# Range checks moved from the recurrence into the second MoE, on a second load

## The chip, the cores and the metric

One core of a Trainium2 chip. The time of a run is the device time of that core in microseconds (us). The engines are TensorE (PE in the profile; PEld are its weight loads), VectorE (DVE), ScalarE (ACT), GpSimd (POOL) and SyncE (SP), which here issues every DMA. All work in float32; matrix products of the two MoEs split each operand into a rounded part and a remainder, so that one product becomes several passes of TensorE.

## The reference, cut to what matters

Three stages follow one another. The first is a recurrence over 768 time steps for 4 x 8 heads with a state of 40 x 40. Then come an MLP with an ELU (here called the first MoE; its weights arrive as 64-bit floats) and a soft mixture of 8 experts.

```python
for t in range(S):                       # recurrence, S = 768
    y[t] = einsum('bhd,bhde->bhe', r[t], state)
    Sa = einsum('bhde,bhe->bhd', state, a[t])
    state = state * w[t] - outer(Sa, b[t]) + outer(v[t], k[t])
h = x @ w_in                             # first MoE: 3072 tokens, 320 -> 2048 -> 320
x = where(h > 0, h, exp(min(h, 0)) - 1) @ w_out
P = sinkhorn(exp(x @ w_gate), 8 rounds)  # second MoE: 8 experts, 320 -> 1024 -> 320
out = sum_e P[:, e] * (relu(x @ w1[e]) @ w2[e])
```

## The kernel before, in words

**The recurrence** works in 24 chunks of 32 time steps. Chunk c loads w and a together as `WA` (`loadw`, line 290), k and b as `KE` (`loadk`), v as `VU` (`loadv`) and r as `rB` and `rO` (`loads2`). `prep` makes the decays of the chunk from w: two clamped copies (lines 315 and 316), two scans on VectorE (319, 325), and on GpSimd the product `aE` of a with them (327). Its last step is a range check of w on ScalarE: `Abs` with a bias and `Relu` with an accumulated sum, in place in the w half of `WA` (338, 339), summed into `wmm`. `WA` has one buffer (chunk 1 has one of its own), so the next load of w waits for the last reader. `E1` to `E4`, `H1` to `H4` and `O1` to `O3b` are matrix products and transposes of a chunk with the copies behind them. `E3` writes a 32 x 32 matrix for each head to memory (`Ad`, four stores, line 384), `LT` loads it back spread over the partitions (392).

**The triangular solve** (`tsolve`, lines 417 and 424) handles two chunks at a time with 62 short VectorE operations (`Tt`, `Wk`). It needs `LT` of both chunks; its result goes through memory again (`Td`, line 430, and `TT`, 434).

**The first MoE** runs unit by unit between the steps of the recurrence: `m1_mm1` (588), an ELU on ScalarE, VectorE and GpSimd, `m1_mm2` (615 to 619). Its weights are converted early on: 16 + 16 tiles, loaded as 64-bit words into two `raw` buffers (211, 221). `to_f32` turns the two 32-bit halves of a float64 into a float32: `Abs` on ScalarE (197), a clamp on VectorE that keeps the exponent in range (198), a shift (199) and two merges with words of the raw tile (200, 201).

**The second MoE** (`phase_b`) is 8 experts x 6 blocks x 8 slices = 384 units: `mm1` (773), `hh` on ScalarE (776), `hl` on VectorE (777), and two units later `mm2` (814 to 816). Weights come through a ring of 11 tiles (`wload`, 732 to 742), three units ahead of their use at a change of expert; one block of x at a time through `xload`. `gates` and `check_w`, which turns `wmm` into the flag, are spread over the first expert's units. At the end the flag selects a general version of the whole computation, which does not run with these inputs.

**What sets the order.** The tile framework orders the instructions of each engine by priority. For the loop over chunks the string `order` in `PLAN` gives the sequence of steps (`prep+4` is the next step of `prep` for chunk c + 4, `m` a unit of the first MoE, `p` three steps of the solve); from c = 4 on each engine follows it exactly. `start` gives the steps ahead of the loop. SyncE issues DMAs in order, so one that waits for a free buffer holds those behind it.

Of the kernel before, what the change touches and what calls it, by code (L numbers as in the profile page):

```python
# [22 lines left out]
PLAN = {  # L23
# [76 lines left out]
def build(ctx, tc, r, k, v, w, a, b, w_in, w_out, wg, w1, w2, wa_d, kb_d, re_d, ro_d, vt_d, wp_d, consts, out, C, off):  # L100
    nc = tc.nc
    B, H, S, D = r.shape
    DM = H * D
    NT = B * S
    NCH = S // C
    NG = H // 2
# [44 lines left out]
    flag = per.tile([1, 1], I32, name="flag")  # L151
    main = ExitStack()
    moe = ExitStack()
    rec = ExitStack()
# [37 lines left out]

    dve = {}

    def to_f32(raw, tmp):
        lo, hi, m = raw[:, :, 0], raw[:, :, 1], tmp.bitcast(I32)
        A.activation(out=tmp, in_=hi.bitcast(F32), func=AF.Abs)
        V.tensor_scalar(out=tmp, in0=tmp, scalar1=XLO, scalar2=XHI, op0=ALU.max, op1=ALU.min)
        V.tensor_scalar(out=m, in0=m, scalar1=3, scalar2=0x3FFFFFF8, op0=ALU.logical_shift_left, op1=ALU.bitwise_and)
# [52 lines left out]
    wmm = per.tile([128, NCH + 2], F32, name="wmm")  # L252
    wmid, whalf = wmm[:, NCH:NCH + 1], wmm[:, NCH + 1:NCH + 2]
    CI = C // 4

    work = {None: (wr, wq, dq, aB)}
# [1 line left out]
    def rec_init():  # L258
        for t in (wr, wq, dr, dq):
            V.memset(t, 0.0)  # L260
        work[1] = (early(1, "wr", [4 * NG, C + 1]), early(1, "wq", [4 * NG, C]), early(1, "dq", [4 * NG, C]), early(1, "aB", [NG * 2 * 2, 64]).rearrange("p (g u j) t -> p g u j t", u=2, j=2))
        for t in work[1]:
            G.memset(t, 0.0)
        V.memset(dr[:, :, 0], 1.0)
        for i in (3, 2):
            V.memset(bank[i], 0.0)
        for t in (aB, wmm, rB, *TTs, Yw):
            G.memset(t, 0.0)
        G.memset(wmid, -(WLO + WHI) / 2)
        G.memset(whalf, 1e-5 - (WHI - WLO) / 2)  # L270
        for i in (0, 1):
            V.memset(bank[i], 0.0)

# [35 lines left out]
    def prep(c):  # L309
        z = st[c]  # L310
        NX = 4 * NG
        wr, wq, dq, z.aB = work.get(c, work[None])
        wf = z.WA[0:HR, 0].rearrange("p g t -> p (g t)")
        wv = wf.rearrange("p (x t) -> p x t", x=NX)
        V.tensor_scalar(out=wr[0:HR, :, 1:C + 1], in0=wv[:, :, ::-1], scalar1=WLO, scalar2=WHI, op0=ALU.max, op1=ALU.min)
        V.tensor_scalar(out=wq[0:HR, :, 1:C], in0=wv[:, :, 0:C - 1], scalar1=WLO, scalar2=WHI, op0=ALU.max, op1=ALU.min)
        yield
        F = early(c, "F", [NX, C + 1])
        V.tensor_tensor_scan(out=flat(F)[0:HR], data0=flat(wr)[0:HR], data1=flat(dr)[0:HR], initial=0.0, op0=ALU.mult, op1=ALU.add)
        z.Wf = r2.tile([128, NX], F32, tag="Wf", name="Wf", bufs=4)  # L320
# [12 lines left out]
        kv = z.KE[0:HR].rearrange("p g u (b k t) -> p (g u b) k t", b=2, k=2)  # L333
        fr = F[0:HR, :, 0:C][:, :, ::-1]
        for kb in range(2):
            G.tensor_tensor(out=kv[:, :, kb, :], in0=kv[:, :, kb, :], in1=fr, op=ALU.mult)
        yield
        A.activation(out=wf, in_=wf, func=AF.Abs, bias=wmid[0:HR])
        A.activation(out=wf, in_=wf, func=AF.Relu, bias=whalf[0:HR], accum_out=wmm[0:HR, c:c + 1])

    def unpad(dst, ps):
        return dst.rearrange("p (j g e) -> p j g e", j=2, g=NG), ps.rearrange("p (g x) -> p g x", g=NG)[:, :, 0:128].rearrange("p g (j x) -> p j g x", j=2)[:, :, :, 0:D]
# [360 lines left out]
    def check_w(c1, px_tile):  # L703
        mm = c1.tile([128, 1], F32, name="mmw")
        V.tensor_reduce(out=mm, in_=wmm[:, 0:NCH], axis=AX.X, op=ALU.add)
        V.tensor_scalar(out=mm, in0=mm, scalar1=0.0, scalar2=None, op0=ALU.is_le)
        yield
        ps = px_tile()
        T.transpose(ps[0:1, 0:128], mm, ident)
        mn = c1.tile([1, 1], F32, name="mnw")  # L710
        V.tensor_reduce(out=mn, in_=ps[0:1, 0:128], axis=AX.X, op=ALU.min)
        V.tensor_scalar(out=mn, in0=mn, scalar1=-1.0, scalar2=1.0, op0=ALU.mult, op1=ALU.add)
        V.tensor_copy(out=flag, in_=mn)
        yield


# [4 lines left out]
    def phase_b(mg):  # L721
# [110 lines left out]
        for i in range(len(units) + LAG):  # L832
            if i < len(units):
                e, bk, f = units[i]
                if e == 0 and f == 2 and bk + 1 < NBLK:
                    xload(bk + 1)
                if i >= 2:
                    mm1(e, bk, f)
            if i >= LAG:
                e, bk, f = units[i - LAG]  # L840
                if gg is not None and e == 1:
                    run_all(gg)
                    gg = None
                mm2(e, bk, f)
                if bk == NBLK - 1:
                    del ring[(e, f)]
                    wnext()
            if gg is not None:
                if next(gg, 1) == 1:
                    gg = None  # L850


    def general():
        with ExitStack() as fx:
# [52 lines left out]
            for i in range(NF1):  # L907
                fs = slice(128 * i, 128 * i + 128)
                es = slice(128 * i * e32, (128 * i + 128) * e32)
                raw = f2.tile([128, 3, 128, e32], I32 if wide else F32, tag="fraw", name="fraw")  # L910
                SY.dma_start(out=raw[:, 0:2].rearrange("p k f e -> p k (f e)"), in_=wi_d[0:256, es].rearrange("(k p) f -> p k f", p=128))
                SY.dma_start(out=raw[0:64, 2].rearrange("p f e -> p (f e)"), in_=wi_d[256:320, es])
                SY.dma_start(out=raw[64:128, 2].rearrange("p f e -> p (f e)"), in_=wi_d[256:320, es])
                rv = raw.rearrange("p k f e -> p (k f) e")
                x = to_f32(rv, f2.tile([128, 384], F32, tag="cv", name="cv")) if wide else rv[:, :, 0]
# [278 lines left out]
```

## Time and profile before

| | us |
|---|---|
| median of 3 runs (lowest, highest) | 2324.01 (2320.37, 2327.19) |
| the profiled execution's own time | 2325.87 |
| its span, first to last instruction | 2323.8 |
| busy: PE, PEld, DVE, ACT, POOL | 2149.5, 1960.3, 989.1, 752.8, 469.2 |
| mean granted TensorE clock | 0.978 |

The span is what the views of the profile cover; the execution's own time is 2 us longer. A row of the timeline gives start, duration, engine, line, operation, the tiles out<-in, and in brackets the idle time ahead of it and what ended that.

### The profile page before, as it was taken

What the parts mean: (1) busy time and instruction counts of PE and PEld (TensorE: products, weight loads), DVE (VectorE), ACT (ScalarE), POOL (GpSimd) and SP (SyncE); (2) the same over time, 40 slices, a digit from 0 to 9 for tenths busy, and PEclk for the clock granted to TensorE, in tenths of its full rate; (3) what the DMA queues carried; (4) which work ended last, traced back from release to release, by engine and by line L of the source; (5) the groups of instructions that cost most, each with busy time, mean ns of one, the idle gap of its engine ahead of it and who ended that gap; (6) DMA issues with size and microseconds to landing.
All of it is one profiled execution on the core that took longest, in us unless ns stands there. A gap on an engine that the chain in (4) does not pass through costs nothing.

```text
span 2323.8 us, 47093 instructions
## 1 busy us (share of the span) xinstructions
PE 2149.5 (93%) x19908; PEld 1960.3 (84%) x19908; DVE 989.1 (43%) x2112; ACT 752.8 (32%) x1663; POOL 469.2 (20%) x556
## 2 busy tenths in 40 slices
PE   2377799999999999999999999999999999999998
PEld 2266788888888998899999999999999999999997
DVE  6788666676777622542222222222222222222222
ACT  3243345555555556323212112112112112112111
POOL 5244133433443326001002002002002002001000
PEclk9987799999999999999999999999999999999999
DMA  6344334433344223101001001001001001000000
GB/s 161 97 134 121 82 95 102 107 100 84 102 107 108 65 53 111 61 1 34 17 1 39 12 1 40 11 1 45 7 1 45 6 1 48 4 1 20 23 24 25
DMA packets 171588, 121.62 MB, mean 52 GB/s; under 512 B 102824, under 2 KB 151336, under 8 KB 171368
## 3 DMA queue, kind: packets, MB, share of 16 engines
q1 hardware_dynamic: 171368, 118.52, 19.0%
q8 instruction: 158, 2.59, 0.5%
q14 instruction: 62, 0.51, 0.1%
HBM read 99.99 MB, written 18.48 MB: 51 GB/s over the span
## 4 chain that ended last, share of the span: by engine, by line
PE 74%; DVE 11%; DMA 8%; SPq 2%; ACT 2%; issue 2%; POOL 1%; DVEq 0%; ACTq 0%; POOLq 0%
PE h L773 30%; PE pa L816 9%; PE pa L815 9%; PE pa L814 9%; PE ph L588 5%; DVE Wk L424 3%; DVE Tt L417 2%; DMA LT<-Ad 2%; PE a L615 2%; DMA Ad<-Am 2%; DMA WA<-in_wa 1%; PE a L616 1%; PE a L617 1%; DMA raw<-in_wp 1%; PE P L545 1%
## 5 line engine op out<-in xcount | busy, mean ns | idle before, releaser
L773 PE MATMUL h<-xs,a 128*128 128x512 f32 x2560 | 640.9, 392 | 0.0
L777 DVE SCALAR_TENSOR_TENSOR hl<-h,hh 128x512 fp32r<-128x512 f32 x384 | 264.8, 690 | 870.2 <-ACT hh L776 869.7
L776 ACT ACTIVATE hh<-h 128x512 fp32r<-128x512 f32 x384 | 229.4, 598 | 1015.3 <-PE h L773 1011.7
L773 PEld LDWEIGHTS h<-xs,a 128*128 128x128 f32 x2560 | 469.1, 188 | 82.7
L815 PE MATMUL pa<-a,hl 128*128 128x320 f32 x1536 | 474.4, 309 | 0.0
L814 PE MATMUL pa<-a,hh 128*128 128x320 f32 x1536 | 472.6, 309 | 0.6 <-ACT logits L643 0.3
L816 PE MATMUL pa<-a,hh 128*128 128x320 f32 x1536 | 468.6, 309 | 0.0
L815 PEld LDWEIGHTS pa<-a,hl 128*128 128x128 f32 x1536 | 289.0, 188 | 15.0
L814 PEld LDWEIGHTS pa<-a,hh 128*128 128x128 f32 x1536 | 289.0, 188 | 14.2 <-ACT acc L821 0.7
L816 PEld LDWEIGHTS pa<-a,hh 128*128 128x128 f32 x1536 | 287.3, 188 | 0.0
L741 POOL TENSOR_TENSOR a<-rw,a 128x384 fp32r<-128x384 f32 x64 | 65.2, 1019 | 1050.7 <-ACT a L739 1037.2
L588 PE MATMUL ph<-X,Wt 128*128 128x256 f32 x1536 | 236.1, 298 | 5.8 <-DVE g L597 5.7
L601 POOL TENSOR_TENSOR gl<-g,gh 128x256 fp32r<-128x256 f32 x192 | 161.8, 843 | 392.8 <-ACT gh L599 302.0
L588 PEld LDWEIGHTS ph<-X,Wt 128*128 128x128 f32 x1536 | 205.3, 198 | 10.9 <-DVE g L597 7.0
L424 DVE TENSOR_TENSOR Wk<-Wk,Tt 128x120 f32<-128x120 f32 (+30 forms) x403 | 160.0, 397 | 9.4 <-DVE Tt L417 0.2
L597 DVE SCALAR_TENSOR_TENSOR g<-m,ph 128x256 f32<-128x256 f32 x192 | 80.0, 416 | 163.0 <-ACT m L591 144.1
L417 DVE TENSOR_TENSOR Tt<-Wk,LT 128x120 f32<-128x120 f32 (+30 forms) x403 | 130.6, 324 | 37.8 <-DMA LT<-Ad 14.2
L825 DVE SCALAR_TENSOR_TENSOR acc<-pa,Pg,acc 128x320 f32<-128x320 f32 x168 | 84.3, 544 | 114.3 <-PE pa L816 114.3
L773 PE MATMUL h<-X,a 128*128 128x512 f32 x512 | 127.8, 392 | 0.0
L599 ACT ACTIVATE gh<-g 128x256 fp32r<-128x256 f32 x192 | 80.0, 417 | 143.9 <-DVE g L597 142.7
L590 ACT ACTIVATE m<-ph 128x256 f32<-128x256 f32 x192 | 73.0, 380 | 140.2 <-PE ph L588 132.8
L773 PEld LDWEIGHTS h<-X,a 128*128 128x128 f32 x512 | 93.7, 188 | 16.7
(173 smaller groups left out, 2437.2 us busy)
## 6 DMA issues: line engine op xcount, KB each, us to landing
LT<-Ad SPq DMA_DIRECT2D x24, 512.0 KB
rw<-in_moe_w SPq DMA_DIRECT2D x64, 160.0 KB
WA<-in_wa SPq DMA_DIRECT2D x24, 416.0 KB
KE<-in_kb SPq DMA_DIRECT2D x24, 416.0 KB
rw<-in_moe_w SPq DMA_DIRECT2D x64, 128.0 KB
VU<-in_vt SPq DMA_DIRECT2D x24, 320.0 KB
raw<-in_wp SPq DMA_DIRECT2D x16, 384.0 KB
raw<-in_moe_w_out SPq DMA_DIRECT2D x16, 320.0 KB
```

What stands on the lines that cost most here:

```text
L417: V.tensor_tensor(out=tv, in0=Wk[:, :, 0:ni, j:j + 1].to_broadcast(sh), in1=LT2[:, :, j, j + 1:C].unsqueeze(2).to_broadcast(sh), op=ALU.mult,)
L424: dve["T"] = V.tensor_tensor(out=Wk[:, :, 0:ni, j + 1:C], in0=Wk[:, :, 0:ni, j + 1:C], in1=tv, op=ALU.subtract)
L588: T.matmul(ph, lhsT=Wt[0:kp, wi, 128 * f:128 * f + 128], rhs=X[0:kp, xi, :], start=(i == 0), stop=(i == 7))
L597: V.scalar_tensor_tensor(out=g, in0=m, scalar=-1.0, in1=ph, op0=ALU.add, op1=ALU.max)
L601: G.tensor_tensor(out=gl, in0=g, in1=gh.bitcast(F32), op=ALU.subtract)
L773: T.matmul(h, lhsT=a1[:, wi, :], rhs=X[bk][:, xi, :], start=(i == 0), stop=(i == 7))
L776: A.activation(out=hh, in_=h, func=AF.Relu)
L777: V.scalar_tensor_tensor(out=hl, in0=h, scalar=0.0, in1=hh.bitcast(F32), op0=ALU.max, op1=ALU.subtract)
L814: T.matmul(o, lhsT=hh[:, ts_], rhs=a2[:, 0, :], start=(f == 0), stop=False)
L815: T.matmul(o, lhsT=hl[:, ts_], rhs=a2[:, 0, :], start=False, stop=False)
L816: T.matmul(o, lhsT=hh[:, ts_], rhs=a2[:, 1, :], start=False, stop=(f == NF2 - 1))
L825: V.scalar_tensor_tensor(out=at, in0=o, scalar=Pg[:, tt, e:e + 1], in1=at, op0=ALU.mult, op1=ALU.add)
```

## The change

The check of w leaves `prep`, and with it `wmm`. The conversion of the weights in the fast path no longer takes the absolute value and no longer clamps; its shift reads the raw word directly (the general version keeps both, as `guard`). A new generator, `check_ranges`, loads w (24 tiles) and the first MoE's weights (32 tiles) a second time during the second MoE and checks them on ScalarE, one step a unit from the second expert on; its result is put on one partition by two small DMAs in place of a transpose on TensorE. In `order` the step `ldw+4` behind `prep+3` becomes `ldw+5` behind O2, and `ldw_6` is added to `start`.

```diff
-"order": "T lv E4 m prep+3 ldw+4 p E3+3 xl m ... YW+1 prep+4 p O2 x m O2 p ..."
+"order": "T lv E4 m p E3+3 xl m ... YW+1 prep+4 p O2 ldw+5 x m O2 p ..."
-"start": "... ld_5 prep_5"
+"start": "... ld_5 prep_5 ldw_6"
...
-    def to_f32(raw, tmp):
+    def to_f32(raw, tmp, guard=False):
         lo, hi, m = raw[:, :, 0], raw[:, :, 1], tmp.bitcast(I32)
-        A.activation(out=tmp, in_=hi.bitcast(F32), func=AF.Abs)
-        V.tensor_scalar(out=tmp, in0=tmp, scalar1=XLO, scalar2=XHI, op0=ALU.max, op1=ALU.min)
-        V.tensor_scalar(out=m, in0=m, scalar1=3, ...)
+        if guard:
+            A.activation(out=tmp, in_=hi.bitcast(F32), func=AF.Abs)
+            V.tensor_scalar(out=tmp, in0=tmp, scalar1=XLO, scalar2=XHI, op0=ALU.max, op1=ALU.min)
+        V.tensor_scalar(out=m, in0=m if guard else hi, scalar1=3, ...)
...
     def prep(c):
...
-        yield
-        A.activation(out=wf, in_=wf, func=AF.Abs, bias=wmid[0:HR])
-        A.activation(out=wf, in_=wf, func=AF.Relu, bias=whalf[0:HR], accum_out=wmm[0:HR, c:c + 1])
...
+    def check_ranges(c1):
+        tiles = [("w", c) for c in range(NCH)]
+        if wide:
+            tiles += [(n, f) for f in range(NF1) for n in ("i", "o")]
...
+        ahead = []
+        for i, (n, x) in enumerate(tiles + [(None, None)] * 2):
+            if n:
...
+                raw = c1.tile([128, 3 * 128 * 2], I32, tag="rchk", name="rchk", bufs=3)[...]
+                SY.dma_start(out=raw[0:rows], in_=wa_d[x][:, 0:size] if n == "w" else wp_d[x] if n == "i" else wo_d[...])
+                ahead.append((n, i, rows, size, raw))
+            yield
+            if len(ahead) > 2 or not n and ahead:
+                n, i, rows, size, raw = ahead.pop(0)
...
+                if n == "w":
+                    src = raw[0:rows]
+                else:
+                    A.activation(out=t, in_=raw.rearrange("p (f e) -> p f e", e=2)[:, :, 1].bitcast(F32), func=AF.Abs)
+                    yield
+                    src = t
+                A.activation(out=t, in_=src, func=AF.Abs, bias=b0)
+                yield
+                A.activation(out=t, in_=t, func=AF.Relu, bias=b1, accum_out=ok[0:rows, i:i + 1])
+                yield
...
-        ps = px_tile()
-        T.transpose(ps[0:1, 0:128], mm, ident)
...
+        SY.dma_start(out=mdr.rearrange("o p -> p o"), in_=mm)
+        SY.dma_start(out=mn[0:1, :], in_=mdr)
...
-        gg = itertools.chain(gates(logits, Pg, c1, px_tile), check_w(c1, px_tile))
+        gg = gates(logits, Pg, c1, px_tile)
+        cg = check_ranges(c1)
...
+            elif i >= NBLK * NF2 + LAG:
+                next(cg, None)
+        run_all(cg)
```

## Rows read from the trace of the kernel before

**Rows 1.** Stretches; us, then busy (count) of PE, PEld, DVE, ACT, POOL; PEclk; DMA.
```profile
85.00:213.00 128.00, 90.20 (x1274) 77.68 (x1274) 105.67 (x273) 54.87 (x132) 61.52 (x84) 0.90 0.45 126
...
265.00:780.00 515.00, 474.53 (x8251) 442.51 (x8250) 356.51 (x829) 276.34 (x698) 197.59 (x228) 0.98 0.38 99
780.00:870.00 90.00, 88.14 (x1540) 83.34 (x1539) 42.80 (x109) 47.01 (x121) 26.27 (x36) 1.00 0.18 45
...
940.00:2323.80 1383.80, 1374.22 (x7652) 1246.36 (x7652) 376.75 (x661) 290.39 (x518) 101.20 (x108) 1.00 0.07 19
```

**Rows 2.** Waits of VectorE, 265 to 780 us; total us, times, longest.
```profile
DVE wr L315 <- DMA WA<-in_wa: 35.1, 15, 5.3
```

**Rows 3.** Waits of TensorE, 265 to 780 us.
```profile
PE P L516 <- DVE X L576: 9.8, 7, 2.5
```

**Rows 4.** Timeline of VectorE: ends and starts of solves, and waits for WA.
```profile
290.33 0.43 DVE L315 TENSOR_SCALAR wr<-WA 104x512 f32<-104x512 f32 x1 [0.86 <-DMA WA<-in_wa]
...
306.19 0.19 DVE L424 TENSOR_TENSOR Wk<-Wk,Tt 128x16 f32<-128x16 f32 x1
...
325.79 0.43 DVE L315 TENSOR_SCALAR wr<-WA 104x512 f32<-104x512 f32 x1 [5.31 <-DMA WA<-in_wa]
...
332.19 0.23 DVE L417 TENSOR_TENSOR Tt<-Wk,LT 128x62 f32<-128x62 f32 x1 [1.44 <-DMA LT<-Ad]
...
693.57 0.19 DVE L424 TENSOR_TENSOR Wk<-Wk,Tt 128x16 f32<-128x16 f32 x1
...
710.87 0.43 DVE L315 TENSOR_SCALAR wr<-WA 104x512 f32<-104x512 f32 x1 [3.02 <-DMA WA<-in_wa]
...
717.70 0.23 DVE L417 TENSOR_TENSOR Tt<-Wk,LT 128x62 f32<-128x62 f32 x1 [1.86 <-DMA LT<-Ad]
...
741.13 0.43 DVE L315 TENSOR_SCALAR wr<-WA 104x512 f32<-104x512 f32 x1 [0.99 <-DMA WA<-in_wa]
...
756.71 0.19 DVE L424 TENSOR_TENSOR Wk<-Wk,Tt 128x16 f32<-128x16 f32 x1
...
779.05 0.23 DVE L417 TENSOR_TENSOR Tt<-Wk,LT 128x62 f32<-128x62 f32 x1 [2.05 <-DMA LT<-Ad]
```

**Rows 5.** Timeline of SyncE's queue in one turnaround.
```profile
513.36 0.44 SPq L290 DMA_DIRECT2D WA<-in_wa  x1
513.84 0.35 SPq L565 DMA_DIRECT2D yt<-yd  x1
...
519.34 0.57 SPq L392 DMA_DIRECT2D LT<-Ad  x1
```

**Rows 6.** The chain that ended last: the last Ad store of two turnarounds.
```profile
708.32 3.77 DMA Ad<-Am
...
772.42 3.04 DMA Ad<-Am
```

**Rows 7.** The chain that ended last, 85 to 213 us, shares by line.
```profile
by line: DMA raw<-in_wp 16.9%; DMA raw<-in_moe_w_out 11.4%; DVE Wk L424 8.6%; DVE Tt L417 7.2%; DVE tmp L201 6.1%; DVE tmp L200 5.9%; issue 5.9%; DVE tmp L198 5.7%; ACT tmp L197 4.5%; DVE F L319 2.3%; POOL aE L327 2.3%; DVE tmp L199 2.2%; D
```

**Rows 8.** Timeline of VectorE: passes of a conversion.
```profile
18.11 1.34 DVE L198 TENSOR_SCALAR tmp<-tmp 128x384 f32<-128x384 f32 x1
...
144.92 0.36 DVE L199 TENSOR_SCALAR tmp<-tmp 128x384 int32<-128x384 int32 x1
145.32 0.56 DVE L200 SCALAR_TENSOR_TENSOR tmp<-raw,tmp 128x384 int32<-128x384 int32 x1
```

**Rows 9.** Groups of ScalarE by form: the checks; busy us, mean ns, idle before.
```profile
L339 ACT ACTIVATE WA<-WA,wmm 104x512 f32<-104x512 f32 x24 | 17.3, 720 | 0.7
L338 ACT ACTIVATE WA<-WA,wmm 104x512 f32<-104x512 f32 x24 | 17.1, 714 | 18.5 <-DVE wq L316 18.5
```

**Rows 10.** Timeline of ScalarE early in the second MoE.
```profile
965.95 1.49 ACT L761 ACTIVATE xs<-xr 128x1536 fp32r<-128x1536 f32 x1 [5.99 <-DMA xr<-x2d]
967.34 0.58 ACT L776 ACTIVATE hh<-h 128x512 fp32r<-128x512 f32 x1
```

**Rows 11.** Waits of TensorE from 940 us on.
```profile
PE pa L814 <- ACT acc L821: 0.2, 1, 0.2
```

**Rows 12.** Timeline of SyncE's queue: two issues of WA, the second held.
```profile
57.33 13.64 SPq L290 DMA_DIRECT2D WA<-in_wa  x2
```

More of the change, by code (lines that the diff above doesn't have):

```diff
@@ L37 @@
 WLO, WHI = 0.42, 2.4
+WMID, WGAP = 16.0, 2.0 ** -14
 XPAD = tuple(280 + 2560 * i + o for i, o in enumerate((0, 0, 256, 528, 896)))
@@ L150, in build @@
     yd = dr1.tile([NCH, 128, 384], F32, name="yd")
-    flag = per.tile([1, 1], I32, name="flag")
+    flag = per.tile([1, 34], I32, name="flag")[:, 0:1]
     main = ExitStack()
@@ L193, in build @@
     dve = {}
-    def to_f32(raw, tmp):
+    def to_f32(raw, tmp, guard=False):
         lo, hi, m = raw[:, :, 0], raw[:, :, 1], tmp.bitcast(I32)
-        A.activation(out=tmp, in_=hi.bitcast(F32), func=AF.Abs)
-        V.tensor_scalar(out=tmp, in0=tmp, scalar1=XLO, scalar2=XHI, op0=ALU.max, op1=ALU.min)
-        V.tensor_scalar(out=m, in0=m, scalar1=3, scalar2=0x3FFFFFF8, op0=ALU.logical_shift_left, op1=ALU.bitwise_and)
+        if guard:
+            A.activation(out=tmp, in_=hi.bitcast(F32), func=AF.Abs)
+            V.tensor_scalar(out=tmp, in0=tmp, scalar1=XLO, scalar2=XHI, op0=ALU.max, op1=ALU.min)
+        V.tensor_scalar(out=m, in0=m if guard else hi, scalar1=3, scalar2=0x3FFFFFF8, op0=ALU.logical_shift_left, op1=ALU.bitwise_and)
         V.scalar_tensor_tensor(out=m, in0=hi, scalar=-0x40000000, in1=m, op0=ALU.bitwise_and, op1=ALU.bitwise_or)
@@ L251, in build @@
     rB = r1.tile([128, NG, 2, 2, 64], F32, name="rB")
-    wmm = per.tile([128, NCH + 2], F32, name="wmm")
-    wmid, whalf = wmm[:, NCH:NCH + 1], wmm[:, NCH + 1:NCH + 2]
     CI = C // 4
@@ L266, in rec_init @@
             V.memset(bank[i], 0.0)
-        for t in (aB, wmm, rB, *TTs, Yw):
+        for t in (aB, rB, *TTs, Yw):
             G.memset(t, 0.0)
-        G.memset(wmid, -(WLO + WHI) / 2)
-        G.memset(whalf, 1e-5 - (WHI - WLO) / 2)
         for i in (0, 1):
@@ L701, in gates @@
             yield
-    def check_w(c1, px_tile):
+    def check_ranges(c1):
+        tiles = [("w", c) for c in range(NCH)]
+        if wide:
+            tiles += [(n, f) for f in range(NF1) for n in ("i", "o")]
+        ok = c1.tile([128, len(tiles)], F32, name="ok")
+        lim = c1.tile([128, 4], F32, name="lim")
+        V.memset(ok, 0.0)
+        for i, x in enumerate((-(WLO + WHI) / 2, 1e-5 - (WHI - WLO) / 2, -WMID, WGAP - WMID)):
+            V.memset(lim[:, i:i + 1], x)
+        yield
+        ahead = []
+        for i, (n, x) in enumerate(tiles + [(None, None)] * 2):
+            if n:
+                rows = HR if n == "w" else 128
+                size = {"w": NG * B * C, "i": 3 * 128, "o": DM}[n]
+                raw = c1.tile([128, 3 * 128 * 2], I32, tag="rchk", name="rchk", bufs=3)[:, 0:size * (1 if n == "w" else 2)]
+                raw = raw.bitcast(F32) if n == "w" else raw
+                SY.dma_start(out=raw[0:rows], in_=wa_d[x][:, 0:size] if n == "w" else wp_d[x] if n == "i" else wo_d[x * 128:(x + 1) * 128, :])
+                ahead.append((n, i, rows, size, raw))
+            yield
+            if len(ahead) > 2 or not n and ahead:
+                n, i, rows, size, raw = ahead.pop(0)
+                t = c1.tile([128, 512], F32, tag="tchk", name="tchk")[0:rows, 0:size]
+                b0, b1 = (lim[0:rows, j:j + 1] for j in ((0, 1) if n == "w" else (2, 3)))
+                if n == "w":
[7 more added lines that the diff above has]
+                A.activation(out=t, in_=t, func=AF.Relu, bias=b1, accum_out=ok[0:rows, i:i + 1])
+                yield
@@ L704, in check_w @@
         mm = c1.tile([128, 1], F32, name="mmw")
-        V.tensor_reduce(out=mm, in_=wmm[:, 0:NCH], axis=AX.X, op=ALU.add)
+        V.tensor_reduce(out=mm, in_=ok, axis=AX.X, op=ALU.add)
         V.tensor_scalar(out=mm, in0=mm, scalar1=0.0, scalar2=None, op0=ALU.is_le)
         yield
-        ps = px_tile()
-        T.transpose(ps[0:1, 0:128], mm, ident)
-        mn = c1.tile([1, 1], F32, name="mnw")
-        V.tensor_reduce(out=mn, in_=ps[0:1, 0:128], axis=AX.X, op=ALU.min)
-        V.tensor_scalar(out=mn, in0=mn, scalar1=-1.0, scalar2=1.0, op0=ALU.mult, op1=ALU.add)
@@ L713, in check_w @@
-        V.tensor_copy(out=flag, in_=mn)
+        mn = c1.tile([128, 128], F32, name="mnw")
+        mdr = dr1.tile([1, 128], F32, name="mdr")
+        SY.dma_start(out=mdr.rearrange("o p -> p o"), in_=mm)
+        SY.dma_start(out=mn[0:1, :], in_=mdr)
+        yield
+        V.tensor_reduce(out=mm[0:1], in_=mn[0:1, :], axis=AX.X, op=ALU.min)
+        V.tensor_scalar(out=mm[0:1], in0=mm[0:1], scalar1=-1.0, scalar2=1.0, op0=ALU.mult, op1=ALU.add)
+        V.tensor_copy(out=flag, in_=mm[0:1])
         yield
@@ L914, in general @@
                 rv = raw.rearrange("p k f e -> p (k f) e")
-                x = to_f32(rv, f2.tile([128, 384], F32, tag="cv", name="cv")) if wide else rv[:, :, 0]
+                x = to_f32(rv, f2.tile([128, 384], F32, tag="cv", name="cv"), True) if wide else rv[:, :, 0]
                 V.tensor_copy(out=wi[:, :, fs], in_=x.rearrange("p (k f) -> p k f", k=3))
@@ L918, in general @@
                 SY.dma_start(out=raw.rearrange("p f e -> p (f e)"), in_=wo_d[fs, :])
-                x = to_f32(raw, f2.tile([128, 384], F32, tag="cv", name="cv")[:, 0:320]) if wide else raw[:, :, 0]
+                x = to_f32(raw, f2.tile([128, 384], F32, tag="cv", name="cv")[:, 0:320], True) if wide else raw[:, :, 0]
                 V.tensor_copy(out=wo[:, i, :], in_=x)
```

4 rows, old and new, of the table PLAN are left out of this document.

## The prediction

> **What bounds the kernel now.** I read the stretches by stage first. From 940 us on, the second MoE keeps TensorE busy for 1374.22 of 1383.80 us at a granted clock of 1.00 [rows 1]; with 384 units (8 experts x 6 blocks x 8 slices) that is 3.6 us a unit, and nothing off TensorE is worth anything there unless it makes TensorE wait. From 780 to 870 us TensorE is busy 98% as well. Before that it is not: 90.20 of 128 us between 85 and 213 us, and 474.53 of 515 us between 265 and 780 us, the recurrence's steady state, where two chunks share one triangular solve on VectorE. So a gain has to come from before 780 us, and it then shifts everything behind it by the same amount.
>
> Next, who waits in the steady state. VectorE stands 35.1 us, 15 times, for the load of w and a (WA) [rows 2]. TensorE's own waits there are mostly for VectorE's work, the largest named one 9.8 us in seven waits [rows 3]. The timeline of VectorE shows where a period goes: the solve ends at 306.19 us and the next one starts at 332.19, when LT lands; the last of seven such gaps is 693.57 to 717.70 [rows 4]. I call this gap the turnaround: 26.0 us in the first, 24.1 us in the last, 24.7 us in the mean of the seven. In between VectorE works through the solve, some 39 us. Turnaround plus solve, about 64 us, is the pace of the stage. The reader should see that the WA waits are of two kinds. The 5.31 us at 325.79 lie inside a turnaround, and VectorE stands another 1.44 us for LT afterwards, so they hide; the 0.99 us at 741.13 lie inside a solve and count in full [rows 4].
>
> **Part 1, w loaded a loop ahead.** WA has one buffer. Its last reader is now the check on ScalarE, so the load goes out early in the loop that needs it. Without the check the last reader is the product aE on GpSimd, and the load goes out half a loop before its use. Of the 15 waits seven are in turnarounds (5.31 us the first, 3.02 the last, 29.5 together) and eight in solves (0.86 the first, 0.99 the last, 5.6 together) [rows 2, 4]. The first kind I cost at nothing: LT hides it, by 1.44 us at the first and 1.86 at the last. The second kind I count in full, 0.7 us a period.
>
> The load is also in the way of LT. On SyncE it is issued at 513.36, in 0.44 us, ahead of the four Ad stores that LT waits for; LT goes out at 519.34 [rows 5]. Moved behind O2 this issue leaves the turnaround: 0.49 us with the gap behind it (the next issue starts at 513.84). And WA no longer shares the DMA engines with Ad: the last Ad store lands in 3.77 us with WA in flight (708.32) and in 3.04 us in the one turnaround that has neither a WA nor a KE load, at 772.42 [rows 6]. That is 0.7 us; with the issue 1.2 us, and I take 1.1. A check on it: that last turnaround, 756.71 to 779.05, lasts 22.3 us against the mean of 24.7 [rows 4], so 2.4 us is the upper end; part of it is KE's, whose load stays. The lower end is the issue alone, 0.5 us. New in its place: SyncE waits after O2 for aE, which was issued some steps earlier; queued behind it there are only the next loop's r loads, and ScalarE, VectorE and TensorE wait for none of these soon. I cost it at nothing; its price would be the old one. Eight periods (seven shown and one around 250 us): 8 x (1.1 + 0.7) = 14.4 us. I take 13, since TensorE has waits of only some 40 us to give in the stage [rows 1]; ends 4 (8 x 0.5) and 23 (8 x 2.4 is 19, and 5.6 on top gives 25; less 2 for TensorE).
>
> **Part 2, conversion without the clamp.** Each of the 32 conversions loses one ScalarE pass and one VectorE pass. On the chain of waits between 85 and 213 us (128 us) these stand for 4.5% and 5.7%, so 5.8 and 7.3 us, 13.1 us together [rows 7]. The raw tiles have two buffers, so a load waits for the conversion two before it, and the chain runs load, ScalarE, four VectorE passes, load. One row changes its form: the shift takes 0.36 us now, in place; the new one reads every second word of the raw tile, which the next pass, with two operands, does in 0.56 us [rows 8]. Its ends are 0.36 and 0.56; I take 0.56, since only that row reads the raw tile. With about 11 conversions on the chain that gives back 2.2 us, so 10.9 us is left. VectorE is 83% busy in this stretch [rows 1], so not all of it is the chain's: I take 8, ends 2 (VectorE sets the pace with other work) and 13.
>
> The Trainium skill speaks against this step: its page Vector Engine (DVE) Microarchitecture Reference, section 5.2, says that a port keeps its full rate only over pairs of adjacent words, and puts one operand that hops every element at 1.73 ns a column, an estimate of 0.74 us here; the term would be some 2 us smaller, 6 in place of 8. The 0.56 us row, 1.5 ns a column with all fixed cost, shows no such penalty.
>
> In the first 85 us five conversions delay the loads of WA behind them on SyncE, among them one clamp pass of 1.34 us at 18.11 [rows 8]. I take 3 us, ends 0 and 4.
>
> **Part 3, the checks in the second MoE.** Removed from the recurrence: 24 pairs of ScalarE passes of 0.71 and 0.72 us [rows 9]; ScalarE is half busy there, so beyond freeing WA I cost them at nothing. Added: 56 tiles, 24 x 2 + 32 x 3 = 144 passes of about that size, some 105 us of ScalarE in a stage where it has 290 of 1383 us [rows 1, 9], and 16.6 MB of loads (24 x 208, 16 x 384 and 16 x 320 KB) where the DMA engines are 7% busy. They cost something only if ScalarE comes late with hh. At 965.95 it stood 5.99 us for a load with hh behind it, and TensorE waited 0.2 us for the ScalarE pass behind it [rows 10, 11]. So I cost them at nothing; the cover is TensorE's lag of two units, 7 us. One transpose on TensorE goes, two tiny DMAs come; under 1 us either way.
>
> **The sum.** 3 + 8 + 13 = 24 us off the profiled execution's own 2325.87 us (span 2323.8 and 2 around it) gives 2302. That execution lies 1.9 us above the median of the runs, 2324.01, so I predict 2300 us.
>
> **Rivals.** *The room is taken by others* (0.17). The conversions are paced by VectorE's other work, and the turnaround by SyncE's Td and TT issues. For it: VectorE's 83%. Against it: the turnaround without WA is in fact shorter. All low ends: 0 + 2 + 4 = 6 us, 2318 on the median; no change.
>
> *The load does not come earlier* (0.11). SyncE reaches it late, or the first loops, whose order is not written out by hand, come out in another order, and WA lands as late as now. Then only the conversions count: 3 + 8 = 11 us, 2313.
>
> *The check loads hold up weights* (0.10), slower. SyncE works in order. A check load whose buffer is not free holds the weight loads queued behind it. What such a hold can last is seen at 57.33, where SyncE stood behind two WA loads for 13.64 us [rows 12]. At each of seven changes of expert the weights run three units, 10.8 us, ahead; filling a tile takes some 5 us by my estimate (a load of 3 to 4 us like the Ad store [rows 6] and two passes of about 0.7). A hold of 13.6 us then costs 13.6 + 5 - 10.8 = 8 us, seven times 56: 2324 - 24 + 56 = 2356. It decides from 3.4 us a change, where it eats the 24. Against it: rows 10 and 11, and a check tile needs only a few passes to free its buffer.
>
> My main case has 0.62.
>
> **How the numbers follow.** About 0.3%, 7 us, is what a measurement of this kernel can tell from no change. Main case and second rival are faster: 0.73. The first rival is no change: 0.17. Slower: 0.10. The main case's own bounds are 24 with ends 6 and 40, so 2284 to 2318; the range takes in the first two rivals wholly and a little noise, 2284 to 2322, and leaves out the slow rival and a little at the fast end.
>
> **What would show it.** Right: VectorE's waits for WA fall from 35.1 us to under 5; turnarounds last about 23.5 us; the solves lose their short WA waits; the last conversion ends some 10 us earlier than now; TensorE's unit stays at 3.6 us. Wrong: turnarounds still near 24.7 us although WA is early; WA still awaited; waits of TensorE for weights or hh after 940 us.

## The result, and the profile after

The changed kernel takes 2301.6 us (median of four runs, 2299.05 to 2303.49); the kernel before, run beside it, 2325.6 us (2320.37 to 2332.15). The ratio is 0.9892 with a 95% interval of 0.987 to 0.9914, so 20 to 30 us are gone, 25 in the middle. The profiled execution took 2300.21 us (span 2298.2), 25.66 us less than the one shown before.

The stretches of the changed kernel, with the columns of [rows 1]:

```profile
0.00:85.00 85.00, 19.09 (x183) 15.02 (x184) 59.64 (x122) 14.40 (x29) 37.72 (x45) 0.72 0.50 132
85.00:213.00 128.00, 90.39 (x1290) 77.49 (x1290) 100.83 (x254) 43.95 (x106) 61.13 (x80) 0.63 0.49 133
...
265.00:780.00 515.00, 490.25 (x8632) 459.38 (x8633) 372.78 (x876) 266.87 (x680) 203.92 (x235) 0.99 0.38 100
...
940.00:2298.00 1358.00, 1349.73 (x7518) 1224.38 (x7516) 364.64 (x639) 356.32 (x682) 100.65 (x106) 1.00 0.10 29
```

Between 265 and 780 us TensorE is busy 490 us in place of 475: the stretch holds more work. ScalarE has lost 10.9 us between 85 and 213 us, and VectorE 4.8; in the second MoE ScalarE has gained 66 us.

VectorE's three longest kinds of wait in the steady state (265 to 745 us) of the changed kernel; there is no row for WA any more, where [rows 2] had 35.1 us:

```profile
DVE g L592 <- ACT m L586: 66.1, 42, 2.8
DVE g L592 <- POOL xT L544: 14.0, 8, 1.8
DVE Am L364 <- PE P L362: 13.7, 8, 1.9
```

What SyncE's queue stood for there, first in the kernel before, then in the changed one:

```profile
SPq L392 <- DMA Ad<-Am: 39.8, 15, 3.8
```

```profile
SPq L288 <- POOL aE L325: 59.5, 14, 5.8
SPq L387 <- DMA Ad<-Am: 16.6, 16, 3.1
```

LT waits 23 us less for the Ad stores. SyncE now stands 59.5 us for aE with the load of w, as foreseen, and no engine's waits name a load that is queued behind it. One turnaround of SyncE's queue, which answers to [rows 5] (the solve ended at 486.03):

```profile
495.80 1.80 SPq L429 DMA_DIRECT2D TT<-Td  x4
497.64 0.45 SPq L405 DMA_DIRECT2D Wk<-in_consts  x1
498.14 1.31 SPq L560 DMA_DIRECT2D yt<-yd  x1
499.50 1.91 SPq L379 DMA_DIRECT2D Ad<-Am  x4
502.75 0.57 SPq L387 DMA_DIRECT2D LT<-Ad  x1
503.42 0.51 SPq L293 DMA_DIRECT2D KE<-in_kb  x1
507.56 0.33 SPq L288 DMA_DIRECT2D WA<-in_wa  x1
508.00 0.35 SPq L298 DMA_DIRECT2D VU<-in_vt  x1
```

From the end of the Ad issues to LT's issue: 1.3 us here. WA goes out at 507.56, just as the next solve starts. On VectorE, the same turnaround (it answers to [rows 4]):

```profile
474.36 0.42 DVE L592 SCALAR_TENSOR_TENSOR g<-m,ph 128x256 f32<-128x256 f32 x1 [1.18 <-ACT m L586]
...
486.03 0.19 DVE L419 TENSOR_TENSOR Wk<-Wk,Tt 128x16 f32<-128x16 f32 x1
...
500.24 0.42 DVE L313 TENSOR_SCALAR wr<-WA 104x512 f32<-104x512 f32 x1
...
507.57 0.23 DVE L412 TENSOR_TENSOR Tt<-Wk,LT 128x62 f32<-128x62 f32 x1 [0.56 <-DMA LT<-Ad]
```

It lasts 21.54 us, and wr finds WA there. The seven turnarounds mean 21.9 us, against 24.7.

Where the 25.6 us came from in this pair of profiles: the first solve of the steady state starts at 257.24 instead of 264.79 (7.6 us); eight periods later it is 752.44 instead of 779.05, so the steady state gave another 19.1; 1.0 us was given back after that.

### The profile page after: what moved, and what is told of

Read it like the earlier page. It is cut to its first block, busy times and chain, and to the rows that moved or that the text cites. A ratio compares the mean times of both kernels' runs of the same rounds, so it can differ in the third digit from the quotient of the medians.

```text
span 2298.2 us, 47292 instructions
## 1 busy us (share of the span) xinstructions
PE 2140.2 (93%) x19907; PEld 1953.3 (85%) x19907; DVE 982.0 (43%) x2085; ACT 792.5 (34%) x1759; POOL 472.9 (21%) x553
## 4 chain that ended last, share of the span: by engine, by line
PE 75%; DVE 11%; DMA 7%; SPq 3%; issue 2%; ACT 1%; POOL 1%; DVEq 0%; ACTq 0%; POOLq 0%
PE h L803 30%; PE pa L847 10%; PE pa L846 10%; PE pa L845 10%; PE ph L583 5%; DVE Wk L419 3%; DVE Tt L412 2%; DMA LT<-Ad 2%; PE a L610 2%; PE a L611 1%; PE a L612 1%; DMA WA<-in_wa 1%; DVE g L592 1%; SPq L429 1%; SPq L425 1%
## 5 line engine op out<-in xcount | busy, mean ns | idle before, releaser
L412 DVE TENSOR_TENSOR Tt<-Wk,LT 128x120 f32<-128x120 f32 (+30 forms) x403 | 135.9, 337 | 43.5 <-DMA LT<-Ad 20.2
```

The source lines that it names most:

```text
L412: V.tensor_tensor(out=tv, in0=Wk[:, :, 0:ni, j:j + 1].to_broadcast(sh), in1=LT2[:, :, j, j + 1:C].unsqueeze(2).to_broadcast(sh), op=ALU.mult,)
```

## The experiments

All runs together. *w*: where its load lies (in: in the turnaround; behind: behind the start of the solve). *First*: start of the first steady-state solve. *Turn*: mean of the next seven turnarounds. *Ad-LT*: mean time in these from the end of the Ad issues to LT's issue. *Eight*: from the first start to that of the eighth next solve. All are us, from each run's timelines of VectorE and SyncE. *Ratio*: time to that of the kernel before on the same chip, with its interval.

```
run                    w       First   Turn   Ad-LT  Eight   Ratio
before                 in      264.79  24.71  3.44   514.26
e12_conv_only          in      258.05  24.91  3.60   523.32  0.9967 [0.9954, 0.9981]
e2b_w_late_pinned      in      254.53  25.06  3.33   522.03  0.9942 [0.9928, 0.9957]
after                  behind  257.24  21.88  1.65   495.20  0.9892 [0.9870, 0.9914]
e1_clamp_back          behind  265.72  22.64  1.56   494.29  0.9921 [0.9894, 0.9948]
e2_w_load_late         behind  255.30  22.52  1.48   505.20  0.9884 [0.9859, 0.9909]
e3_one_check_tile      behind  257.57  22.01  1.54   495.50  0.9905 [0.9881, 0.9929]
e4_before_no_w_check   behind  267.45  22.37  1.38   501.80  0.9899 [0.9882, 0.9916]
e5_copy_in_turnaround  behind  265.37  22.87  1.53   501.12  0.9942 [0.9923, 0.9961]
e6_tiny_in_turnaround  behind  257.75  23.06  1.43   507.73  0.9906 [0.9880, 0.9933]
e5b_copy_pinned        behind  260.17  24.16  2.55   513.32  0.9987 [0.9976, 0.9998]
e6b_tiny_x4_pinned     behind  263.42  26.62  1.78   525.79  1.0031 [1.0019, 1.0043]
e11b_tt_behind_lt      behind  255.34  21.10  2.09   485.79  0.9858 [0.9835, 0.9880]
e11_solve_before_xy    behind  255.69  23.99  1.91   509.49  0.9947 [0.9931, 0.9964]
```

Seven rows (after, e1, e2, e3, e4, e5, e6) have the same steady state but for details, and three have w in its turnarounds (before, e12, e2b). Their means are 22.5 against 24.9 us of turnaround, 1.51 against 3.46 us from Ad to LT, 500 against 520 us for eight periods. Single profiles of the same steady state differ by up to 13 us there, so one pair of them would not have settled a few microseconds. The ratios come from medians, *First* to *Eight* from one execution each: that of e2b was the longest of its six (2328.1 us, their median 2318.3), that of e12 lay 5.6 us above its median and that of e2 7.0.

### The conversion, undone and alone

Undone (e1):

```diff
-    def to_f32(raw, tmp, guard=False):
+    def to_f32(raw, tmp, guard=True):
```

> The changed kernel with one part undone: each conversion has its ScalarE Abs and its VectorE clamp again. Theory A (the recurrence, not the conversions, paces the first 265 us; the conversion part is worth only what that stretch gained beyond the load of w, some 3.5 to 7 us): 2305 to 2309 us, first steady-state solve starts at 260 to 264 us instead of 257.24, turnarounds after it stay near 21.9 us. Rival B (the conversions are worth the 11 us that the prediction gave to the two early terms): 2312 to 2314 us, that solve starts at about 268.

The first solve starts at 265.72, 8.5 us later than in the changed kernel, and turnarounds stay at 22.6. The time (0.9921) lies 0.3% above it: some 7 us, with overlapping intervals. So neither holds whole: 0.9921 of 2325.6 us is 2307, as theory A had it, and the start lies between the two, nearer to rival B. No run gave the 11 us. Alone, in the kernel before (e12):

```diff
-    def to_f32(raw, tmp):
+    def to_f32(raw, tmp, guard=False):
...
-        V.tensor_scalar(out=m, in0=m, scalar1=3, scalar2=0x3FFFFFF8, ...)
+        if guard:
+            A.activation(out=tmp, in_=hi.bitcast(F32), func=AF.Abs)
+            V.tensor_scalar(out=tmp, in0=tmp, scalar1=XLO, scalar2=XHI, op0=ALU.max, op1=ALU.min)
+        V.tensor_scalar(out=m, in0=m if guard else hi, scalar1=3, scalar2=0x3FFFFFF8, ...)
```

> The kernel before with the new conversion alone: no Abs, no clamp, the shift reads the raw tile; w is checked in the recurrence as before and its load stays in the turnaround; the 64-bit weights are not range checked. Theory A (the two parts are separate: conversion some 8 us before 265 us, load of w some 17 us in the steady state): the first steady-state solve starts at 254 to 258 us instead of 264.79; turnarounds 24.5 to 25.2 us and eight periods 512 to 522 us as in the two runs that have w there; ratio 0.995 to 0.998. Rival L (the early time is given back before the steady state ends, or it needs the early load too): first start 262 us or later, or eight periods over 522 us, ratio 0.998 to 1.001.

First start 258.05, ratio 0.9967: 0.33% of 2330 us, 7.7 us faster (4 to 11), as theory A had it. The eight periods, 523.3 us, lie over the 522 from which rival L would count; beside 522.0 in e2b and 514.3 in the profile before, and in an execution above the run's median, I take that for spread. VectorE's waits for WA and SyncE's for Ad, 265 to 745 us of this run, are close to those of the kernel before:

```profile
DVE wr L316 <- DMA WA<-in_wa: 38.0, 15, 5.3
...
SPq L393 <- DMA Ad<-Am: 47.9, 18, 4.4
```

So the two parts are separate. With the old conversion the first start is at 264.79, 265.72 and 267.45 (before, e1, e4), with the new one at 255.3 to 258.1 in six runs with no other change before it (after, e2, e3, e11b, e11, e12): about 9 us.

### What moves the load of w

First its entry in the order was put back, from behind O2 to the early place (e2):

```diff
-    "order": "T lv E4 m p E3+3 ... p O2 ldw+5 x ...",
+    "order": "T lv E4 m ldw+4 p E3+3 ... p O2 x ...",
-    "start": "... prep_5 ldw_6",
+    "start": "... prep_5",
```

> The changed kernel with the load of w put back to its old place early in the loop that needs it; no w check in the recurrence. Theory A (the gain of the steady state is the load's place): turnarounds back to 24 to 25 us, VectorE's waits for WA back to 30 us or more, time 2318 to 2322. Rival C (what helped is that the two ScalarE check passes are gone and free WA earlier): turnarounds stay at 22 to 23 us, time 2301 to 2306.

Both numbers fell to rival C, but for a reason that neither named: the load did not move. In the two traces all 928 issues of SyncE stand in the same order, and so do the instructions of every other engine; WA (445.25) goes out behind LT (441.21):

```profile
441.21 0.56 SPq L387 DMA_DIRECT2D LT<-Ad  x1
441.88 0.51 SPq L293 DMA_DIRECT2D KE<-in_kb  x1
445.25 0.33 SPq L288 DMA_DIRECT2D WA<-in_wa  x1
```

The written order holds TensorE, VectorE, ScalarE and GpSimd (PINNED lists these four); DMA issues on SyncE are placed by the scheduler, by when their buffer comes free. So e2 is a second sample of the changed kernel. The next run has the load of w held at the old place (e2b; the issue of w gets an order edge behind that of Wk, or rO, and the first Ad store one behind w):

```diff
+                    if n == "ldw" and c >= 4 and c + o < NCH:
+                        dve["X"] = traced()[-1]
+                        tc.add_manual_dep(dve['X'], (dve['R'] if c % 2 else dve['K']).name, NoSync ...)
```

> The changed kernel with the load of w at its old place, and this time held there: in SyncE's queue it stands behind the load of Wk (or of rO in the loops without a turnaround) and ahead of the Ad stores. The range check of w stays in the second MoE. Theory A (the load's place in the turnaround is what the steady state paid for): the seven turnarounds mean 24 to 25 us, where the four runs that load it late in the loop have 21.9 to 23.1; eight periods take 512 to 518 us where those have 494 to 508; ratio to before 0.993 to 0.997. Rival C (the check passes themselves were the price): turnarounds 22 to 23, ratio 0.987 to 0.990.

Turnarounds 25.06 us, eight periods 522, ratio 0.9942: the ratio is theory A's, no check pass being in the loop, and the two others lie a little above its ranges. VectorE waits for WA again (265 to 745 us):

```profile
DVE wr L313 <- DMA WA<-in_wa: 29.4, 7, 5.0
```

The place in the turnaround is not the whole price, though. By the ratios e2b lies some 12 us above the changed kernel and e2 (0.9942 against 0.9892 and 0.9884), and some 6 us below e12 (0.9967), which has the same conversion and the old recurrence with its check; the second difference is barely clear of the intervals. What e2b did not put back is the check passes, and the late load in the loops without a turnaround: there WA goes out well ahead of the Ad stores, and of the 15 waits only the seven in turnarounds are back. Which of the two makes the rest is not shown, so rival C is not excluded for it.

And the kernel before without the check of w, its order untouched (e4):

```diff
-        A.activation(out=wf, in_=wf, func=AF.Abs, bias=wmid[0:HR])
-        A.activation(out=wf, in_=wf, func=AF.Relu, bias=whalf[0:HR], accum_out=wmm[0:HR, c:c + 1])
+        pass
+        pass
```

> The kernel before without the range check of w (its two ScalarE passes a chunk are left out and w is not checked at all); the text of the order is not touched, the conversions keep their clamp. Without the check the load of w has the product on GpSimd as its last reader. Theory F (the place of the load follows from its readers, the order's entry is not needed): WA goes out behind the solve's start, eight periods 494 to 508 us, the first steady-state solve still starts near 264 us, ratio 0.992 to 0.996. Rival G (the entry in the order does the move): turnarounds near 24.7, VectorE's waits for WA near 35 us, ratio 0.998 to 1.002.

Theory F, and beyond its 0.992 to 0.996: two lines removed give 0.9899, nearly the whole change. A turnaround of this run:

```profile
451.75 1.91 SPq L384 DMA_DIRECT2D Ad<-Am  x4
454.87 0.56 SPq L392 DMA_DIRECT2D LT<-Ad  x1
455.53 0.51 SPq L295 DMA_DIRECT2D KE<-in_kb  x1
458.38 0.33 SPq L290 DMA_DIRECT2D WA<-in_wa  x1
```

The load went behind LT by itself, because its buffer's last reader is now the product on GpSimd. The first start, 267.45, shows that this gives nothing before 265 us.

### What a transfer in the turnaround costs

Two runs were to put a copy of w (e5) or 512 bytes of it (e6) at the old place of the load, by an entry in the order:

```diff
-    "order": "T lv E4 m p E3+3 ...
+    "order": "T lv E4 m dl p E3+3 ...
+    def loadx(c):
+        x = drp.tile([128, 2 * NG * B * C], F32, tag="dum", name="dum", bufs=2)
+        SY.dma_start(out=x[0:HR], in_=wa_d[c])
```

In e6 the last line is

```diff
+        SY.dma_start(out=x[0:1, 0:128], in_=wa_d[c][0:1, 0:128])
```

> The changed kernel with one more transfer of 416 KB, from device memory to device memory, issued in each loop where the load of w was issued before, ahead of the Ad stores; nothing reads it. Theory A (sharing the DMA engines with Ad and LT is most of the price): landing of the last Ad store and of LT longer by 1.8 and 0.3 us or more, turnarounds 24 to 25 us, time 2318 to 2324 although WA is never waited for. Rival D (the price was VectorE's arrival at a late WA): only the issue counts, turnarounds 22.4, time 2304 to 2307.

> The same as the run with the copy of 416 KB, but 512 bytes of one row are copied. Theory A: only the issue of about 0.5 us in SyncE's queue counts, turnarounds near 22.4 us, time 2303 to 2307 (at most 8 x 0.5 = 4 us more). Rival E (a place in the queue is what costs, whatever its size): turnarounds near 24 us, time 2315 to 2320.

Neither tested it. For the same reason as in e2 all 22 copies went out early, between 14.5 and 48.1 us in e5. Its first solve starts 8 us late (265.37), where e6 with its small copies starts at 257.75; the turnarounds of both (22.9 and 23.1 us) are those of the changed kernel. The copies were then held between the load of Wk and the Ad stores in nine turnarounds by order edges as in e2b, one of 416 KB in e5b, four of 512 bytes in e6b:

```diff
+                elif n == "dl":
+                    if c >= 4 and c % 2 == 0 and c + 3 < NCH:
+                        for _ in range(1):
+                            x = loadx()
+                            tc.add_manual_dep(x, dve.get('X', dve['K']).name, NoSync ...)
+                            dve["X"] = x
```

(range(4) and the small copy in e6b.)

> The changed kernel with one copy of 416 KB, device memory to device memory, held in SyncE's queue between the load of Wk and the Ad stores in nine turnarounds; nothing reads it and w is still early. Theory A (the issue and the shared DMA engines are the price): last Ad store to LT 1.5 us longer or more, turnarounds 24 to 25 us, eight periods 512 to 518 us, ratio 0.993 to 0.998. Rival D (the price was VectorE waiting for a late WA): turnarounds at most 0.5 us longer, 22.4 to 23.4, ratio 0.988 to 0.991.

Theory A by turnarounds and eight periods: 24.16 us, 1.7 longer than the mean of 22.5, and 513 us, though w is early and never awaited. Two of its numbers were missed: from Ad to LT it takes 1.0 us more and not 1.5, and the ratio, 0.9987, lies above its range. By the ratios the copies cost some 23 us, and the profile shows about 13 of them in the eight periods and about 4 ahead of these; where the rest lies is open. The Ad stores start 0.8 us later (14.86 us after the solve's end, against 14.08 in the mean of the seven runs), and from Ad to LT it takes 1.0 us more (2.55 against 1.51).

> The same place, with four copies of 512 bytes each: about 2 us of issues ahead of the Ad stores, next to no bytes. If every microsecond that SyncE spends ahead of the Ad stores lengthens the turnaround: 24.3 to 25 us each, ratio 0.994 to 0.997. If the turnaround has slack there (VectorE's own passes end last): under 1 us each, 22.6 to 23.5 us, ratio 0.989 to 0.992.

This went beyond both expectations: 26.6 us, 4.1 longer. One turnaround of SyncE's queue (the solve ended at 499.63):

```profile
511.32 0.45 SPq L410 DMA_DIRECT2D Wk<-in_consts  x1
511.81 3.20 SPq L297 DMA_DIRECT2D dum<-in_wa  x4
515.05 0.58 SPq L565 DMA_DIRECT2D yt<-yd  x1
515.73 1.85 SPq L384 DMA_DIRECT2D Ad<-Am  x4
517.68 0.38 SPq L293 DMA_DIRECT2D KE<-in_kb  x1
518.84 0.60 SPq L392 DMA_DIRECT2D LT<-Ad  x1
```

The four issues hold SyncE's queue for 3.2 us here, and for 2.5 to 3.3 in the nine turnarounds, though next to no bytes move; one of them takes 0.59 us (median), as does a copy of 416 KB in e5b. The mean start of the Ad stores is 2.6 us later. The scheduler also put KE ahead of LT, and LT then takes 6.3 us from its issue to the start of the solve in place of 4.8. The turnaround has little slack on SyncE: what is issued ahead of Ad counts nearly in full, and VectorE's row for LT rose from 6.4 us in the changed kernel to

```profile
DVE Tt L417 <- DMA LT<-Ad: 38.1, 7, 6.3
```

### The checks in the second MoE

In the changed kernel, 900 to 1100 us, ScalarE's groups of the check, and TensorE's two longest waits between 870 and 1100 us:

```profile
L730 ACT ACTIVATE tchk<-tchk,lim 104x512 f32<-104x512 f32 (+2 forms) x56 | 36.1, 645 | 1.1
...
L728 ACT ACTIVATE tchk<-tchk,lim 128x384 f32<-128x384 f32 (+1 forms) x32 | 18.9, 590 | 0.8
L728 ACT ACTIVATE tchk<-rchk,lim 104x512 f32<-104x512 f32 x24 | 17.3, 723 | 2.5 <-DMA rchk<-in_wa 2.0
L725 ACT ACTIVATE tchk<-rchk 128x384 f32<-128x384 f32 (+1 forms) x32 | 16.6, 520 | 0.8
```

```profile
PE pa L846 <- DVE hl L807: 2.4, 2, 1.2
PE pa L845 <- ACT acc L852: 2.1, 1, 2.1
```

All 144 passes lie there, not spread over the experts, and TensorE waits 4.5 us for hl and acc. e3 takes nearly all of them out:

```diff
-        tiles = [("w", c) for c in range(NCH)]
-        if wide:
+        tiles = [("w", 0)]
+        if False:
```

> The changed kernel with the range checks in the second MoE cut to the first of the 56 tiles (the other 55 are not checked). Theory H (the checks cost what TensorE waits for hl and acc around the start of the second MoE): those waits of 4.5 us go, the stretch from the last solve to the end is 2 to 4 us shorter than the 1511 to 1514 us of the runs with all checks, ratio 0.985 to 0.988. Rival I (hidden wholly): 1511 to 1514 us, ratio 0.988 to 0.990.

The waits for hl and acc are gone, but another has taken their place. With one tile to check, the flag's two small DMAs come early, and VectorE stands for the second of them ahead of a step of the gate (m1r) that TensorE needs:

```profile
932.13 0.27 DVE L741 TENSOR_REDUCE mmw<-mnw 1x1 f32<-1x128 f32 x1 [10.22 <-DMA mnw<-mdr]
932.34 0.27 DVE L672 TENSOR_REDUCE m1r<-px 1x1 f32<-1x128 f32 x1
```

```profile
PE px L675 <- DVE m1r L672: 6.6, 1, 6.6
```

In the changed kernel the same wait of VectorE takes 7.78 us, at 1056.14, and TensorE has no wait near it.

From the last solve's end (787.51) to the end it took 1518.1 us, and 0.9905 is no gain. So the run doesn't price the checks. Another count does: that stretch takes 1510.3, 1508.5 and 1508.7 us in the three profiles without checks there (before, e4, e12), and 1510.8 to 1516.0 in the ten that have all of them: 1509.2 and 1512.7 in the mean. That is about 3.5 us, and TensorE's waits account for it: in that stretch those for hl and acc come to 1.9 to 4.6 us in each of the ten, 3.2 in the mean, and to 0.2 at most in the three.

### A faster version

If SyncE's issues ahead of the Ad stores set the turnaround, others can go too. e11b puts the second chunk's four TT loads and the load of rO behind LT, with order edges:

```diff
-            for bb in range(B):
-                bi = bb % 2
-                SY.dma_start(out=z.TT[...], in_=Td[...])
+            if not (x and c >= 6):
+                loadT(c)
-    "order": "... E2+3 LT+3 m ...
+    "order": "... E2+3 LT+3 tt ro m ...
```

> The changed kernel with SyncE's queue shortened ahead of the Ad stores: the four TT loads of the second chunk and the load of rO stand behind LT from the third solve on. Theory A (SyncE's issues ahead of the Ad stores lengthen the turnaround): LT goes out 1.5 to 2.5 us earlier, at 15 to 16 us after the solve's end, and the turnaround falls until VectorE's own passes end last, 20.5 to 21.3 us in place of 22.5; eight periods 485 to 495 us; ratio 0.982 to 0.986. Rival J (the second chunk's TT is now late and holds the loop behind it): turnarounds shorter but solves or TensorE's waits longer by the same, eight periods 495 to 508 us, ratio 0.987 to 0.991.

Turnarounds 21.1 us, eight periods 485.8, ratio 0.9858 [0.9835, 0.988]: theory A; 33 us off the kernel before, and the shortest eight periods of all profiles, though from the fastest of its six executions. The intervals of the ratios still overlap a little with the changed kernel's two (after and e2), so the step beyond it, some 7 us, is barely clear of noise. A turnaround of SyncE's queue (the solve ended at 475.58):

```profile
486.40 0.41 SPq L418 DMA_DIRECT2D Wk<-in_consts  x1
487.20 1.23 SPq L572 DMA_DIRECT2D yt<-yd  x1
488.52 1.87 SPq L382 DMA_DIRECT2D Ad<-Am  x4
491.59 0.56 SPq L390 DMA_DIRECT2D LT<-Ad  x1
492.20 2.07 SPq L405 DMA_DIRECT2D TT<-Td  x4
```

LT goes out 16.0 us after the solve's end, and 16.1 in the mean of seven, against 17.7 in the seven runs above. Five of these turnarounds last 20.88 to 20.95 us: there VectorE comes straight from Y to the solve. The last run also put the solve's first passes ahead of X and Y (e11):

```diff
-    "order": "... prep+4 p H3 m G x H3 p ...
+    "order": "... prep+4 G p H3 m x p H3 p ...
```

> The same, and the solve's first passes stand ahead of X and Y on VectorE, so that LT alone sets the start. Theory A: turnarounds 18.5 to 20 us, eight periods 470 to 488 us, ratio 0.973 to 0.982. Rival K (TensorE, busy 490 of 515 us in this stage, sets the pace before that): eight periods 485 to 500 us, ratio 0.983 to 0.989, with VectorE's and ScalarE's waits for TensorE up by what the turnaround lost.

It is slower, and neither theory had it: turnarounds 24.0, eight periods 509.5. The solve now ends earlier in the written order, so more of the loop's other steps lie between its end and the next start; the Ad stores start 15.2 us after the end, against 11.8 in e11b. Whether another place would do better is open.

## Why the prediction was right, and where it was not

The time (2300 against 2301.6) and the direction were right, and so was the cause: the load of w leaves the turnaround because its buffer loses its last reader. The terms were less good than their sum: the steady state came out 7 us larger than forecast, the conversion 2 to 3 smaller, and the checks took back 3.5 that stood at nothing. That these errors nearly cancel is luck.

**Steady state: 13 us predicted, 20 measured** (520 against 500 us for eight periods). The step that was mis-sized is the price of sharing the DMA engines with Ad. I put it at 0.7 us, from the one turnaround that had neither WA nor KE in flight [rows 6]; measured, from Ad to LT, it is 1.95 (3.46 against 1.51); whether the stores share the engines' rate with the load or stand behind it there, no run tells. That turnaround was a poor measure: the changed kernel's last one has neither load either and still takes 3.25 us from Ad (745.59) to LT (748.84); why is open. The turnaround as a whole fell by 2.4 us, my upper end. In e5b issue and transfer of a copy of the same size, within device memory, make 1.7 us, with no one waiting for the data. The ratios agree with some 20 us: e4 against the kernel before gains 23, and the changed kernel against e12 17, or 21 without what its checks cost. Putting the load back into the turnaround lost some 12 of these (e2b); what makes the rest stays open.

**The short waits for WA inside the solves** I counted in full, 0.7 us a period. They went and were replaced. The kernel before, and in the same place of the changed kernel the row at 474.36 shown above:

```profile
484.18 0.43 DVE L315 TENSOR_SCALAR wr<-WA 104x512 f32<-104x512 f32 x1 [1.14 <-DMA WA<-in_wa]
```

1.14 us for WA became 1.18 us for ScalarE's m. The eight solves of a profile sum to 322.8 us in the mean of the three runs with w in the turnaround and 320.2 in that of the seven others, which differ among themselves by 11 us. The difference of 2.6 us is less than the 5.6 that I counted, but this spread does not tell it from either 5.6 or nothing.

**TensorE's limit.** I cut the term to 13 since TensorE had some 40 us of waits to give [rows 1]. It gave 15.7 (490.25 against 474.53); its 9.8 us for X at the O1 step [rows 3] went entirely. The cut had no row behind it.

**The order's entry.** "Moved behind O2 this issue leaves the turnaround" gave the entry what the missing reader does (e2, e4).

**Conversion and the first 85 us: 11 predicted, 8 to 9 measured** (7.7 by e12's ratio, 9 by the first start). The direction held; the mechanism did so in part. The conversions themselves end 26 us earlier (the last shift starts at 168.8 in place of 195.2, below), where I looked for some 10. Only 8 to 9 us of that reach the first solve of the steady state: 88 us lie between that shift and this solve's start, in place of 70. So it is not the conversions that end last there: the chain just ahead of 257.24 runs through the solve before and the transfers Td, TT, Ad and LT. That 11 came near 8 to 9 does not bear out the shares of the chain [rows 7]. One row inside it was wrong: the shift, which I took at 0.56 us for reading every second word. Before, in place, and after, from the raw tile (ns, min/median/max of 32):

```profile
L199 DVE TENSOR_SCALAR tmp<-tmp x32: 292/348/1412, 16.8 to 195.2; 128x384 int32<-128x384 int32 x16, 128x320 int32<-128x320 int32 x16
```

```profile
L201 DVE TENSOR_SCALAR tmp<-raw x32: 296/349/1366, 16.7 to 168.8; 128x384 int32<-128x384 int32 x16, 128x320 int32<-128x320 int32 x16
```

It costs nothing more. The estimate of 0.74 us from the Trainium skill's Vector Engine (DVE) Microarchitecture Reference, section 5.2, does not hold for this pass: the row of 1.73 ns a column that it used was measured on an operation with two operands and hops of 4 KiB, and this pass has one operand that steps over every second word. The measurement decides. With 0.36 the conversion term would have been 2 us larger by my own working, and further off.

**The checks: 0 predicted, about 3.5 us measured.** TensorE's lag did not cover the start of the second MoE, where 144 passes came together and hl and acc came late (3.2 us of waits). The two tiny DMAs cost next to nothing, as forecast, only because TensorE's lag covered the 7.8 us that VectorE stood for them; in e3 it did not, and TensorE waited 6.6 us.

**The rivals.** *The room is taken by others* fell: the turnaround shortened by its upper end. But its mechanism is what sets the turnaround that is left: four TT issues and one of rO moved out of it gave another 1.4 us a turnaround (e11b). *The load does not come earlier* fell in the steady state. *The check loads hold up weights* fell: from 940 us on TensorE's only listed wait is 2.1 us, for ScalarE's copy of acc, and none for weights. TensorE's pace there is the old one, 5.54 matmuls a us (7518 in 1358.00) against 5.53 [rows 1].

By their ratios the parts add up: e12 and e4 together make 0.9967 x 0.9899 = 0.9866, and the whole change, whose checks e4 does not have, 0.9892 and 0.9884; the 4 to 6 us between agree with the 3.5 us of the checks, though these intervals would not tell that from nothing.

## What to carry to other kernels

Before costing a moved DMA, look whether its queue follows the written order at all: here the last reader of a buffer placed the load, and taking away two passes that no other engine waited for moved it. Price the room ahead of a dependent store and load over many repeats of the gap, not by the one odd gap that happens to lack the transfer. In a gap that is all one queue's issues, count issues as well as bytes; and the next step is to move the others behind it. A profile is one execution: compare its time with the run's median before its stages are summed.

## What the runs showed of the hardware

The issue of a copy within device memory took SyncE 0.59 us in the median, of 416 KB (nine in e5b) as of 512 bytes (36 in e6b). Four of the small ones lengthened the turnarounds more than one of 416 KB did (4.1 against 1.7 us, part of it by KE's new place).

Single executions of seven kernels with nearly the same steady state spread from 494 to 508 us over eight periods; the changed kernel and e2, whose traces have one order on every engine, lie 10 us apart there (495.2 and 505.2).

TensorE's granted clock, a mean of its two levels of 1.2 and 2.4 GHz, was 0.72 in the first 85 us of the changed kernel, and 1.00 in that of e2, whose instructions have the same order; the stretch to 213 us has 0.63 and 0.88. The rows of e2 (those of the changed kernel stand above):

```profile
0.00:85.00 85.00, 21.11 (x208) 16.78 (x208) 60.04 (x122) 14.57 (x29) 37.73 (x45) 1.00 0.51 135
85.00:213.00 128.00, 90.15 (x1283) 77.22 (x1282) 102.39 (x259) 43.96 (x106) 61.16 (x80) 0.88 0.50 134
```

Six of the profiles have the lower clock there and eight the higher one, with no part of the change to tell them apart, and the first solve of the steady state starts 2 us apart (257.24 and 255.30). The chain of waits of this stretch has loads, VectorE and ScalarE as its largest parts, not TensorE [rows 7]; why the clock differs is open.
